# Three edits to the order of copies, sums and loads in a linear-attention plus feed-forward kernel

## The chip, the cores and the metric

The kernel runs on one core of one Trainium2 chip. The metric is the device time of one execution in microseconds (us); lower is better. Times below are from the runs of the kernel before the change and from the hardware profile of one of its executions.

## The reference

Inputs are q, k and v of shape (4, 8, 768, 64): 4 batches, 8 heads, 768 tokens, 64 channels. Two weight matrices follow, `w_in` (512 x 2048) and `w_out` (2048 x 512). All are float32. Cut to what matters:

```python
# linear attention with one decay gamma[h] per head
for t in range(768):
    state = gamma * state + k[:, :, t] outer v[:, :, t]
    y[:, :, t] = (q[:, :, t] @ state) / 8
# 4*768 = 3072 tokens, 8*64 = 512 channels
x = y.transpose(0, 2, 1, 3).reshape(3072, 512)
h = maximum(x @ w_in, 0)
out = (h * h) @ w_out            # (3072, 512)
```

## The kernel before, in words

**Chunks and blocks.** The tokens are cut into 24 chunks of 128. In the attention, a chunk's scores (its keys against its queries, masked) are multiplied with v, and the state of all earlier chunks is added. q and k are scaled by powers of gamma beforehand, so that the recurrence becomes plain products. The result of a chunk, transposed, is `xt`, the input of the feed-forward part. That part works on blocks: `BLOCKS = [4, 2, 2, ...]` gives block 0 four chunks and the ten others two each. The code calls a block `tb`.

**Products of a block.** First `psf <- xt, w_in_bf` (line 850), eight or sixteen matmuls into one PSUM tile. Then ScalarE (ACT in the profile) writes `h` with a ReLU out of PSUM (line 859), and VectorE (DVE) squares it in place (line 830, or ACT at line 828). Last come the products with `w_out`.

**Seven products instead of eight.** For blocks 1 to 10, and for the second half of block 0, the products with `w_out` are made as a 2 x 2 split with seven half-size products (Winograd's variant of Strassen's method). DVE makes sums of quarters of the squared `h`, called `s1` to `s4`; sums of quarters of `w_out` (`t1` to `t4`, the tiles `w_sum`) are made once. The products go to the accumulators `pa`, `pb`, `pd` and `pe`. `a` is a copy of `pa`'s first product. `u` is `pb + a`, `v` is the same after a further product has been added to `pb`, and the output halves are built from these by DVE adds or ACT copies into the tiles `osb` (`oa` and `ob` in the code). `seven_products` does this for blocks 1 and up; its `add` is line 883 and its matmuls are line 887. `last_of_first` does it for tokens 256 to 511 of block 0; its `add` is line 1007 and its matmuls are line 1011. There `pa` and `pe` are the two halves of one PSUM tile, `pd` and `pb` of another. Tokens 0 to 255 of block 0, chunks 0 and 1, are multiplied plainly (line 1045) into the two tiles `ops`; `store(c)` copies `ops[c]` to an `osb` tile on ACT (line 1073) and issues its output DMA on the queue of SyncE (SP, line 1074).

In `last_of_first`, the copy of `pa`'s final sum into `oa` is line 1086. In `seven_products`, `s4` lies in the space of `h` for block 1 (the tile is called `h2` and shows as `h<-h,h`) and in the tile `v_bd0` for later blocks (`v_bd<-h,k_bd`). Only `last_product` reads `s4`; it is put off into the next block (`kept`), where one step multiplies and two steps store.

**Who decides the order.** Nothing is scheduled by a planner. Each engine runs its instructions in the order of the program. The feed-forward part is a row of generators; every `yield` is a "place" with a number. At each place, `before(n)` runs the attention steps that `put(place, step, ...)` has placed there. A block of two chunks has 16 places. The waits between engines are semaphores that the framework sets from the tiles that instructions read and write.

**Attention from chunk 8 on** (`attend2`). With `d` the place of a chunk's outputs, a pair of chunks' q is loaded at `d - 29` (`load_q`, line 94), scaled at `d - 19` and `d - 18` by DVE (`scale_q`, line 390, `qs<-qn`), and transposed by DMA at `d - 16` (line 446). v is scaled at `d - 9` by DVE (`scale_v2`, line 721, shown as `v<-stage,kf`) and copied by GpSimd (POOL, line 729); k is transposed by DMA at `d - 13` (line 735). State products (`c_ps`, line 778) come at about `d - 6` and `d - 3`, scores (`st`, line 751) at `d - 5`, outputs (`y`, lines 800 and 807) at `d`. Chunks 4 to 7 take an older path: k is transposed on TensorE (line 433) and copied to `k_bd` by ACT (line 440), scores are line 459 with their mask on DVE at line 466, state copies are lines 510 (ACT) and 512 (DVE), and outputs are lines 527 and 535.

**Loads of q.** `load_q(m, heads)` issues one DMA on SP for each part of the heads that it is given. Two parts are given for chunks 6, 8 and 10, and one part, all eight heads, for chunks 12, 14, 16, 18, 20 and 22:

```python
for part in heads:
    src = q[b, part, i * C : (i + 2) * C, :].rearrange("h (s r) d -> s h r d", r=2)
    nc.sync.dma_start(t[:, part], src)
```

Of the kernel before, what the change touches and what calls it, by code (L numbers as in the profile page):

```python
# [14 lines left out]
ALU = mybir.AluOpType  # L15
# [16 lines left out]
def kernel(  # L32
# [12 lines left out]
    B, H, S, D = q.shape  # L45
# [51 lines left out]
    heads_of = [slice(0, H // 2), slice(H // 2, H)]  # L97
# [766 lines left out]
    def seven_products(tb):  # L864

        h = h2s[tb][0].rearrange("e (j k) (c t) -> e k c j t", k=2, c=2)
        a11, a12, a21, a22 = h[:, 0, 0], h[:, 1, 0], h[:, 0, 1], h[:, 1, 1]
        s1, s2, s4 = (
            t.rearrange("s p hh d -> s (p hh d)").rearrange("s (j t) -> s j t", t=C)
            for t in (k_bds[0], k_bds[1], v_bds[0])  # L870
        )
        if tb == 1:
            room = hpool.tile([P, 4096], BF16, name="h2").rearrange("e (n j t) -> e n j t", n=4, t=C)
            s1, s2, s4 = (room[:, n] for n in range(3))
        s3 = a21
        t1, t2, t3, t4 = sums
        b11, b21, b22 = (
            lambda j, k=k, n=n: w_out_bf[j // 2][:, 2 * (j % 2) + k, n * HN : (n + 1) * HN]
            for k, n in ((0, 0), (1, 0), (1, 1))
        )  # L880

        def add(out, in0, in1, op=ALU.add):
            nc.vector.tensor_tensor(out=out, in0=in0, in1=in1, op=op)  # L883

        def product(to, left, right, js, start, stop):
            for j in js:
                nc.tensor.matmul(  # L887
                    to,
                    lhsT=left[:, j],
                    rhs=right(j) if callable(right) else right[:, j],  # L890
                    start=(start and j == 0),
                    stop=(stop and j == NFB // 2 - 1),
                    skip_group_check=True,
                )

        def first_sums(js):
            add(s1[:, js], a21[:, js], a22[:, js])
            add(s2[:, js], s1[:, js], a11[:, js], ALU.subtract)

        def rest():  # L900
            first_sums(slice(4, 8))
            pa = (ps_f if tb == 1 else ps_tp).tile([P, HN], FP32, name="psf" if tb == 1 else "tp")
            pb, pe, pd = (ps_f.tile([P, HN], FP32, name="psf") for _ in range(3))
            oa, ob = (opool.tile([P, DM], FP32, name="osb") for _ in range(2))
            a, u, v = (upool.tile([P, HN], FP32, name=f"u{i}") for i in range(3))
            r0 = first[tb] * C
            for js, stop in ((range(0, 6), False), (range(6, 8), True)):
                product(pa[:], a11, b11, js, True, stop)
                product(pe[:], a22, t4, js, True, stop)
                if stop:  # L910
                    nc.scalar.activation(a[:], pa[:], AF.Copy)
                yield
            add(s3, a11, a21, ALU.subtract)
            product(pd[:], s1, t1, range(8), True, True)
            yield
            add(s4, a12, s2, ALU.subtract)
            product(pb[:], s2, t2, range(8), True, True)
            add(u[:], pb[:], a[:])
            yield
            for js in (range(0, 4), range(4, 8)):  # L920
                product(pa[:], a12, b21, js, False, js[-1] == 7)
                if js[0]:
                    nc.scalar.activation(oa[:, 0:HN], pa[:], AF.Copy)  # L923
                yield
            for js in (range(0, 4), range(4, 8)):
                product(pb[:], s3, t3, js, False, js[-1] == 7)
                if js[0]:
                    add(v[:], pb[:], a[:])
                    add(ob[:, HN:DM], pd[:], v[:])
                    add(ob[:, 0:HN], pe[:], v[:])  # L930

                    def last_product():
                        product(pd[:], s4, b22, range(8), False, True)
                        add(oa[:, HN:DM], pd[:], u[:])
                        yield
                        nc.sync.dma_start(out[r0 + C : r0 + 2 * C], ob[:])
                        yield
                        nc.sync.dma_start(out[r0 : r0 + C], oa[:])
                        yield

                    kept.append(last_product())
                yield

        def rest_at_end():
            first_sums(slice(4, 8))
            pe, pb, pd = (ps_f.tile([P, HN], FP32, name="psf") for _ in range(3))
            pa, p2 = ps_tp.tile([P, HN], FP32, name="tp"), ps_st.tile([P, HN], FP32, name="st")
            p7 = ps_y.tile([P, HN], FP32, name="y")
            oa, ob = (opool.tile([P, DM], FP32, name="osb") for _ in range(2))
            a, u, v = (upool.tile([P, HN], FP32, name=f"u{i}") for i in range(3))  # L950
            r0 = first[tb] * C
            for js, stop in ((range(0, 6), False), (range(6, 8), True)):
                product(pa[:], a11, b11, js, True, stop)
                product(pe[:], a22, t4, js, True, stop)
            nc.scalar.activation(a[:], pa[:], AF.Copy)
            yield
            add(s3, a11, a21, ALU.subtract)
            product(p2[:], a12, b21, range(0, 4), True, False)
            product(pb[:], s2, t2, range(8), True, True)
            add(u[:], pb[:], a[:])  # L960
            yield
            add(s4, a12, s2, ALU.subtract)
            product(p7[:], s3, t3, range(8), True, True)
            add(v[:], p7[:], u[:])
            add(ob[:, 0:HN], pe[:], v[:])
            yield
            product(pd[:], s1, t1, range(8), True, True)
            add(u[:], pd[:], u[:])
            add(ob[:, HN:DM], pd[:], v[:])
            nc.sync.dma_start(out[r0 + C : r0 + 2 * C], ob[:])  # L970
            yield
            product(p2[:], a12, b21, range(4, 8), True, True)
            add(oa[:, 0:HN], p2[:], a[:])
            for c in range(2):
                cols = slice(c * C, (c + 1) * C)
                p3 = (ps_tp if c else ps_c).tile([P, C], FP32, name="tp" if c else "c_ps")
                product(p3[:], s4, lambda j: b22(j)[:, cols], range(8), True, True)
                to = slice(HN + c * C, HN + (c + 1) * C)
                add(oa[:, to], p3[:], u[:, cols])
                done = slice(HN + c * C if c else 0, HN + (c + 1) * C)  # L980
                nc.sync.dma_start(out[r0 : r0 + C, done], oa[:, done])
            yield

        return first_sums, rest if tb + 1 < len(BLOCKS) else rest_at_end

    def last_of_first():

        def halves_of(k, c):
# [6 lines left out]
        s1, s2, s4 = (  # L995
            [
                t.rearrange("e (x j t) -> e x j t", x=2, t=C)[:, x]
                for x in range(2)
            ]
            for t in (spare[:, i * HN * 4 : (i + 1) * HN * 4] for i in range(3))  # L1000
        )
# [29 lines left out]
        def second_products():  # L1031
# [39 lines left out]
            def store(c):  # L1071
                osb = opool.tile([P, DM], FP32, name="osb")
                nc.scalar.activation(osb[:], ops[c][:], AF.Copy)
                nc.sync.dma_start(out[c * C : (c + 1) * C], osb[:])
# [4 lines left out]
            product(pb, s2, t2, hi)  # L1079
            add(u[:], pb, a[:])  # L1080
            yield
            store(1)
            product(pa, a12, b(1, 0), lo, False)
            yield
            product(pa, a12, b(1, 0), hi, False)
            nc.scalar.activation(oa[:, 0:HN], pa, AF.Copy)
            yield
            product(pb, s3, t3, lo, False)
            yield
# [203 lines left out]
    def put(place, what, *args):  # L1293
        parts.setdefault(place, []).append((what, args))
# [66 lines left out]
    for m, d in zip(range(PACK_FROM, NCHUNK), done):  # L1361
        attend2(m, d, done[m - PACK_FROM - 1] if m > PACK_FROM else 0,
                *ahead.get(m, (d - 19, d - 16, d - 13, d - 9)))
        if m >= 12 and m % 2 == 0:
            put(d - 29, load_q, m)
    places = {
        (8, "k"): [26 + j // 2 for j in range(8)],
        (8, "v"): [35 + j // 2 for j in range(8)],
# [52 lines left out]
```

## Time and profile before

| what | value |
| --- | --- |
| median of 3 runs | 202.81 us (202.81 to 202.84) |
| profiled execution | 202.86 us, of which 201.09 us are its span |
| TensorE busy | 194.7 us, 2361 matmuls, 2361 weight loads |
| VectorE busy | 151.0 us, 327 instructions |
| ScalarE busy | 128.0 us, 260 instructions |
| GpSimd busy | 81.9 us, 154 instructions |
| DMA | 36.03 MB in 92299 packets, 179 GB/s mean |
| granted TensorE clock | 1.00 throughout |

In the profile, PE is TensorE's matmuls and PEld its weight loads, which overlap them; DVE is VectorE, ACT ScalarE, POOL GpSimd, SP SyncE. A line of a timeline gives the start, the time from the first start to the last end, the engine, the line of the code, the operation, the tile written and the tiles read, the shape, and how many instructions are merged; brackets give the idle time of the engine before it and what ended it. A line of the DMA issues gives the tiles, the issuing queue, how often, the size of one and the median time from issue to landing. Matmuls are pipelined: one starts before the end of the one before it is recorded.

### The profile page before, as it was taken

How to read it: one execution, taken by the hardware profiler on the slowest of the kernel's cores; microseconds unless marked ns; L12 is line 12 of the kernel's file. 1: busy time of each engine (PE TensorE's matmuls, PEld its weight loads, DVE VectorE, ACT ScalarE, POOL GpSimd, SP SyncE). 2: the span in 40 equal slices, each digit the busy share in tenths (PEclk: the TensorE clock that was granted, in tenths of full speed). 3: DMA queues.
4: the chain of work that ended last, by engine and by line, in shares of the span. 5: the costliest groups of instructions: out<-in, count | busy, mean ns of one | idle time of the engine just before them, and what ended most of it. 6: DMA issues, size and time to landing. Idle time of an engine off the chain costs nothing.

```text
span 201.1 us, 5856 instructions
## 1 busy us (share of the span) xinstructions
PE 194.7 (97%) x2361; PEld 164.6 (82%) x2361; DVE 151.0 (75%) x327; ACT 128.0 (64%) x260; POOL 81.9 (41%) x154
## 2 busy tenths in 40 slices
PE   7799999999999999999999999999999999999992
PEld 2478445779988999899999999999999999999881
DVE  3987899799698896687697697697696696484472
ACT  8885875264853676774766866864865865845710
POOL 8664760899930762154522185116362202200000
PEclk9999999999999999999999999999999999999999
DMA  5999999999988999598998399989899552101102
GB/s 168 355 375 397 345 191 193 231 229 224 313 176 190 169 229 177 165 138 177 186 181 188 115 169 231 210 195 132 148 175 182 173 93 65 71 0 51 56 0 106
DMA packets 92299, 36.03 MB, mean 179 GB/s; under 512 B 68592, under 2 KB 88304, under 8 KB 92272
## 3 DMA queue, kind: packets, MB, share of 16 engines
q1 hardware_dynamic: 73136, 31.47, 65.1%
q0 software_dynamic: 19136, 4.20, 23.0%
q8 instruction: 18, 0.29, 0.6%
q14 instruction: 9, 0.07, 0.1%
HBM read 27.26 MB, written 6.29 MB: 167 GB/s over the span
## 4 chain that ended last, share of the span: by engine, by line
PE 91%; DVE 3%; DMA 2%; ACT 1%; issue 1%; DVEq 0%
PE psf L850 42%; PE psf L887 21%; PE tp L887 7%; PE psf L1045 3%; PE psf L1011 2%; DMA qn<-in_q_dram 2%; PE st L751 2%; PE y L807 2%; PE y L800 2%; PE c_ps L778 2%; PE c_ps L656 1%; PE y L535 1%; PE st L459 1%; DVE qs L562 1%; PE y L371 1%
## 5 line engine op out<-in xcount | busy, mean ns | idle before, releaser
L850 PE MATMUL psf<-xt,w_in_bf 128*128 128x256 bf16 (+2 forms) x864 | 92.3, 261 | 0.0
L850 PEld LDWEIGHTS <-w_in_bf 128*128 128x128 bf16 x864 | 70.7, 98 | 11.2
L859 ACT ACTIVATE h<-psf 128x512 bf16<-128x512 f32 x96 | 56.3, 595 | 23.5 <-PE psf L850 21.2
L729 POOL COPY v_bd<-v 64x512 bf16<-64x512 bf16 x32 | 21.7, 677 | 76.2 <-DVE v L721 75.3
L830 DVE TENSOR_TENSOR h<-h 128x512 bf16<-128x512 bf16 x80 | 33.0, 428 | 18.5 <-ACT h L859 18.1
L887 PEld LDWEIGHTS <-h 128*128 128x128 bf16 x344 | 31.7, 98 | 3.7 <-issue 0.2
L157 POOL DMA_DIRECT2D k_big<-in_k_dram x40 | 26.6, 686 | 0.0
L887 PE MATMUL psf<-w_sum,h 128*128 128x256 bf16 x168 | 23.5, 273 | 0.0
L887 PE MATMUL tp<-w_out_bf,h 128*128 128x256 bf16 x136 | 19.1, 273 | 0.0
L887 PE MATMUL psf<-w_sum,k_bd 128*128 128x256 bf16 x144 | 17.9, 273 | 0.0
L883 DVE TENSOR_TENSOR u<-psf,u 128x256 f32<-128x256 f32 x20 | 8.5, 424 | 12.3 <-PE psf L887 11.4
L883 DVE TENSOR_TENSOR osb<-psf,u 128x256 f32<-128x256 f32 x29 | 11.5, 421 | 6.6 <-PE psf L887 6.3
L887 PEld LDWEIGHTS <-k_bd 128*128 128x128 bf16 x144 | 13.8, 98 | 1.5
L787 ACT ACTIVATE s_bd<-c_ps 64x256 bf16<-64x256 f32 x29 | 10.7, 369 | 6.3 <-PE c_ps L778 6.3
L390 DVE TENSOR_TENSOR qs<-qn,qf 128x512 bf16<-128x512 f32 x20 | 13.7, 690 | 0.0
L788 ACT ACTIVATE s_bd<-c_ps 64x256 bf16<-64x256 f32 x29 | 11.0, 379 | 0.4
L721 DVE TENSOR_TENSOR v<-stage,kf 128x512 bf16<-128x512 f32 x16 | 10.9, 684 | 0.3 <-issue 0.3
L758 DVE TENSOR_TENSOR pt<-st,cmask 128x512 bf16<-128x512 f32 x16 | 11.0, 688 | 0.2
L923 ACT ACTIVATE osb<-tp 128x256 f32<-128x256 f32 x8 | 3.1, 384 | 12.2 <-PE tp L887 12.2
L814 ACT ACTIVATE xt<-y 128x512 bf16<-128x512 f32 x16 | 9.6, 598 | 1.8 <-PE y L807 1.2
L828 ACT ACTIVATE h<-h 128x512 bf16<-128x512 bf16 x16 | 10.1, 629 | 0.5
L883 DVE TENSOR_TENSOR k_bd<-h 128x512 bf16<-128x512 bf16 x18 | 9.9, 552 | 0.3
(148 smaller groups left out, 290.0 us busy)
## 6 DMA issues: line engine op xcount, KB each, us to landing
out_dram<-osb SPq DMA_DIRECT2D x23, 256.0 KB, 2.5
qn<-in_q_dram SPq DMA_DIRECT2D x9, 512.0 KB, 5.4
stage<-in_v_dram SPq DMA_DIRECT2D x32, 96.0 KB, 4.0
stage<-in_moe_w_in_dram SPq DMA_DIRECT2D x4, 512.0 KB, 6.8
stage<-in_moe_w_in_dram SPq DMA_DIRECT2D x2, 1024.0 KB, 10.7
w_out_bf<-in_moe_w_out_dram POOLq DMA_DIRECT2D x4, 512.0 KB, 10.2
kn<-in_k_dram SPq DMA_DIRECT2D x6, 256.0 KB, 5.7
qn<-in_q_dram SPq DMA_DIRECT2D x6, 256.0 KB, 5.8
```

Of the source, the lines that this page charges most:

```text
L157: nc.gpsimd.dma_start(t[rows, 2 * at_w : 2 * (at_w + size), p, hh, :], half_rows(k, b, 2 * p + hh, i + w, size),)
L390: engine.tensor_tensor(out=out, in0=by, in1=table[:, :, None].to_broadcast([P, H, D]), op=ALU.mult)
L721: nc.vector.tensor_tensor(out=v2.rearrange("s (u p) d -> s u p d", u=2), in0=vn, in1=kf2[:, i, :, :, None].to_broadcast([P, 2, NPAIR, D]), ...
L729: nc.gpsimd.tensor_copy(v_bd[rows, :, hh, :], v2[rows])
L758: nc.vector.tensor_tensor(out=pt[:], in0=st[:], in1=cmask2.rearrange("s r t -> s (r t)")[:, None, :].to_broadcast([P, 2 * NPAIR, C // 2]), ...
L787: nc.scalar.activation(s_bd[halves[0], :, 0, :], c[halves[0]], AF.Copy)
L788: nc.scalar.activation(s_bd[halves[1], :, 1, :], c[halves[1]], AF.Copy)
L830: nc.vector.tensor_mul(hv, hv, hv)
L850: nc.tensor.matmul(hp, lhsT=w_in_bf[g][:, cb, fq * 128 : (fq + 1) * 128], rhs=xts[tb][:, cb, cols], start=(cb == 0), stop=(cb == NCB - 1),)
L859: nc.scalar.activation(hv, hp[:], AF.Relu)
L883: nc.vector.tensor_tensor(out=out, in0=in0, in1=in1, op=op)
L887: nc.tensor.matmul(to, lhsT=left[:, j], rhs=right(j) if callable(right) else right[:, j], start=(start and j == 0), stop=(stop and j == NF ...
```

## The change

There are three edits. In `seven_products`, the sum `s4` is made one step later, behind `pb`'s product, the add of `u` and a `yield`. In `last_of_first`, `store(1)` moves one step later, behind the two parts of `pa`'s last product and the copy of `pa`. q of chunks 12 to 20 is loaded with two DMAs of four heads each; that of chunk 22 still with one.

```diff
@@ seven_products, rest() @@
             add(s3, a11, a21, ALU.subtract)
             product(pd[:], s1, t1, range(8), True, True)
             yield
-            add(s4, a12, s2, ALU.subtract)
             product(pb[:], s2, t2, range(8), True, True)
             add(u[:], pb[:], a[:])
             yield
+            add(s4, a12, s2, ALU.subtract)
             for js in (range(0, 4), range(4, 8)):
                 product(pa[:], a12, b21, js, False, js[-1] == 7)
@@ last_of_first, second_products() @@
             product(pb, s2, t2, hi)
             add(u[:], pb, a[:])
             yield
-            store(1)
             product(pa, a12, b(1, 0), lo, False)
             yield
             product(pa, a12, b(1, 0), hi, False)
             nc.scalar.activation(oa[:, 0:HN], pa, AF.Copy)
+            store(1)
             yield
             product(pb, s3, t3, lo, False)
@@ placing of the attention steps @@
         if m >= 12 and m % 2 == 0:
-            put(d - 29, load_q, m)
+            put(d - 29, load_q, m, heads_of if m < 22 else (slice(0, H),))
```

On the engines' queues this does the following. ACT has `pa`'s copy ahead of chunk 1's copy. DVE has `s4` behind `u` in blocks 1 to 9: in block 1 also behind the mask of a chunk's scores and a copy of the state, in block 2 also behind a scaling of v, in blocks 3 to 8 ahead of that scaling. SP issues five DMAs more; the stores keep their places among its other instructions. The matmuls keep their order.

## The prediction

> **What bounds the kernel now.** I read the page's busy times first, then the chain that ended last, then the timeline of single engines wherever TensorE (PE) did not start matmuls back to back.
>
> ```profile
> span 201.1 us, 5856 instructions
> PE 194.7 (97%) x2361; PEld 164.6 (82%) x2361; DVE 151.0 (75%) x327; ACT 128.0 (64%) x260; POOL 81.9 (41%) x154
> PE 91%; DVE 3%; DMA 2%; ACT 1%; issue 1%; DVEq 0%
> ```
>
> PE is the bound: 97% busy and 91% of the chain, at a granted clock of 1.00. The view by windows gives PE 15.00 of every 15.00 us from 75 to 195 us and 14.98 from 60 to 75. But "busy" hides short stops. A 256-column matmul is recorded with 273 ns, while the chain gives 0.87 us to eight of them, so one can start every 0.109 us; PE may pause some 0.16 us and still look busy. The pauses must be read from starts. After the first 21 us there are only two that the edits can reach; each is followed by the engine that ended it.
>
> First, the timeline around 44 us, in the last part of the first block:
>
> ```profile
> 44.20 0.49 PE L459 MATMUL st<-qT,k_bd 128*128 128x128 bf16 x4
> 44.32 0.60 ACT L1073 ACTIVATE osb<-psf 128x512 f32<-128x512 f32 x1
> 44.53 1.31 PE L1011 MATMUL psf<-w_sum,h 128*128 128x256 bf16 x8
> 44.73 0.69 DVE L466 TENSOR_TENSOR pt<-st,cmask 128x512 bf16<-128x512 f32 x1 [0.27 <-PE st L459]
> 44.82 0.38 ACT L1086 ACTIVATE osb<-psf 128x256 f32<-128x256 f32 x1
> 45.25 0.31 PEld L1011 LDWEIGHTS <-h 128*128 128x128 bf16 x3 [0.29 <-issue]
> 45.68 0.39 PE L459 MATMUL st<-qT,k_bd 128*128 128x128 bf16 x4
> ```
>
> Eight L1011 matmuls take 1.31 us here and 1.04 at 41.79. Four (pb) start at 44.53 and every 0.109 after; the next four (pe) are due at 44.97 and start at 45.25. They share a PSUM tile with pa, whose copy is L1086, and that copy stands on ScalarE (ACT) behind the 0.60 us of chunk 1's copy, L1073. It ends at 45.20, and PE goes on at 45.25.
>
> Second, 61 us, the seven products of block 1:
>
> ```profile
> 61.09 0.69 DVE L883 TENSOR_TENSOR h<-h,h 128x1024 bf16<-128x1024 bf16 x1
> 61.09 1.05 PE L887 MATMUL psf<-w_out_bf,h 128*128 128x256 bf16 x8
> 61.69 0.42 DVE L883 TENSOR_TENSOR u<-psf,u 128x256 f32<-128x256 f32 x1
> 62.02 0.68 DVE L466 TENSOR_TENSOR pt<-st,cmask 128x512 bf16<-128x512 f32 x1
> 62.16 0.60 PE L887 MATMUL psf<-w_sum,h 128*128 128x256 bf16 x4
> ```
>
> The eight on pa start at 61.09 and the last at 61.87 (61.09 + 1.05 - 0.27). The next group writes pb again, is due at 61.98 and starts at 62.16: it must wait until u has been read out of pb (62.11). That u stands on VectorE (DVE) right behind the 0.69 us of s4, the first row.
>
> **The change, part by part.** *Chunk 1's copy behind pa's.* Each is one ACT instruction; none is added. pa's copy now follows k_bd (which ends at 44.30), so it runs 44.32 to 44.70, before PE is due at 44.97. Gain: 45.25 - 44.97 = 0.28. What is late next is DVE: the second scores (45.68 before) would come at 44.97 + 4 x 0.109 = 45.40, but they overwrite st, which the mask add reads until 44.73 + 0.69 = 45.42. From DVE's end to PE's start the trace shows 0.05 (u 62.11 to 62.16), so they start at 45.48: 0.08 given back, net 0.20. Further on, PE arrives 0.20 earlier than before: its transposes of the second half of qs are due at 46.82 against qs ready at 46.62, the last product at 47.94 against pd's reader ending at 47.76. Both hold. Chunk 1's copy now ends near 45.24; its PSUM buffer is wanted by the second group of block 1's first products at 47.04, its store on the SP queue is not reached before 45.78, and its place there is unchanged. The next work on ACT starts at 47.00. So nothing waits for it.
>
> *s4 one step later, block 1.* u starts where s4 did, at 61.09 (its product ends before 60.7), and ends at 61.51, well ahead of PE. Gain 0.18. The mask add and the copy behind it come earlier too; s4 runs near 62.5 and is first read at 65.48.
>
> *s4, blocks 2 to 9.* No PE pause is there to win, so the cover is what counts. In block 2, and in block 9 which loads no v, nothing urgent stands behind s4. In blocks 3 to 8 the v of a later chunk does (rows of block 4):
>
> ```profile
> 105.64 0.69 DVE L883 TENSOR_TENSOR v_bd<-h,k_bd 128x1024 bf16<-128x1024 bf16 x1
> 106.58 0.42 DVE L883 TENSOR_TENSOR u<-psf,u 128x256 f32<-128x256 f32 x1 [0.26 <-PE psf L887]
> 106.92 0.68 DVE L721 TENSOR_TENSOR v<-stage,kf 128x512 bf16<-128x512 f32 x1
> 108.53 0.28 PE L778 MATMUL c_ps<-v,k_big 128*128 128x64 bf16 x4
> 108.73 0.43 DVE L883 TENSOR_TENSOR u<-psf,u 128x256 f32<-128x256 f32 x1 [1.12 <-PE psf L887]
> ```
>
> s4 (first row) moves to 106.92, so v starts 0.60 later, at 107.52, and ends at 108.20. L778 multiplies that v at 108.53. With 0.05 to get there 0.28 is left: no cost, but a thin cover. The v sum at 108.73 waits for PE in any case, and POOL's copies of v, 0.60 later, are read at 115.1. The last product reads s4 at 110.6.
>
> *q by halves, five times.* Bytes and 512-byte pieces stay; SP issues five DMAs more. An issue of half a q takes 0.58 (two in 1.17 at 57.83), of a whole one 0.57 to 0.64, so what stands behind on SP (v loads, transposes of k) comes up to 0.6 later:
>
> ```profile
> qn<-in_q_dram SPq DMA_DIRECT2D x9, 512.0 KB, 5.4
> stage<-in_v_dram SPq DMA_DIRECT2D x32, 96.0 KB, 4.0
> qn<-in_q_dram SPq DMA_DIRECT2D x6, 256.0 KB, 5.8
> kT<-k_big SPq DMA_TRANSPOSE x16, 4.3
> ```
>
> The tightest q is the one issued at 104.68: whole, it lands 4.9 later, at 109.6, and is scaled at 112.04. Scaling needs both halves, so nothing is won either. From below the second half costs nothing (the pairs at 57.83 landed after 3.8 each); from above it takes 7.3, as the pair at 42.85 did: 105.3 + 7.3 = 112.6, against 112.04 less 0.385. DVE idles 0.48 before 113.20 and 0.79 before 115.62, which takes up that lateness. I take zero. The k transpose behind it (106.33) is wanted only at 118.6.
>
> Sum: 0.20 + 0.18, with unrounded rows 0.385 us. The profiled execution took 202.86, of which 201.09 span and 1.77 around it; it would become 202.48. The median of the runs is 202.81, 0.05 below, which gives **202.42**. From 62.2 us on PE has no pause that could take the gain back, and the last block's tail hangs on PE's end.
>
> **The rivals.** *More is won.* Two short waits stand beside the two: k_bd's second half holds PE 0.10 at 44.35, and a square of h about 0.07 at 57.45. If the wait at 45.48 does not arise (0.08), or one of these shrinks as the engines realign, the time is 202.25 to 202.35. For: DVE and ACT there follow PE. Against: k_bd itself is not moved.
>
> *Only one gain stays.* If u is held by something that the rows do not name, or DVE, almost without idle time from 53 to 62 us, does not follow the 0.20, one term drops out: 202.61 or 202.63; both gone, 202.81. This is also the case in which an edit doesn't do what it says.
>
> *v too late (slower).* Place: L778 in blocks 3 to 8. It decides once DVE loses over 0.28 between u and the end of v. For: at 92.49, where v waits for seven DMAs, the trace has 0.33 idle ahead of it. Against: it is there once only, and runs beside u. Were it behind s4 in all six blocks, v would start 0.33 after s4's end instead of 0.09 before, and reach PE at 108.67: 0.14 each, 0.84 in all, 202.42 + 0.84 = 203.27.
>
> *q too late (slower).* Were the second half to take 11.5, the longest of the L94 loads, it would land at 116.8, 5.1 late, and 1.27 idle would leave 3.9 on the path: 206.3. Against: from 71 us on these loads take 4.9 to 6.0. The Trainium skill speaks for it: "DMA: Bandwidth & Descriptors", section "Anatomy of one DMA", gives every transfer a fixed 2.0 us or so besides its bytes. Counted whole, that is an estimate of 109.6 + 0.6 + 2.0 = 112.2 for the second half, which would still leave the sum as it is. The pairs at 57.83 show no such doubling.
>
> **How the numbers follow.** Both stops gone, 202.42 to within 0.05: 0.62. More won: 0.20. One or both terms lost: 0.10. v late 0.05, q late 0.03. A change of 0.2%, about what a measurement of this kernel can tell from none, is 0.41 us, the time 202.40: the main case lies on that edge, and I split it 0.30 below and 0.32 above. Faster: 0.30 + 0.20 = 0.50; same: 0.32 + 0.10 = 0.42; slower: 0.08. The range leaves out the slow cases and the outermost of the others: 202.22 to 202.75.
>
> **What would show it.** Right: ACT has pa's copy before the second L1073, the eight L1011 matmuls at 44.53 take 1.04, the second scores start near 45.48, pb's matmuls follow those on pa without a pause near 61.8, every later stage lies 0.385 earlier, span 200.70; in blocks 3 to 8 v starts 1.0 after u and L778 has no wait; 16 q loads of 256 KB and four of 512. Wrong: a pause ahead of L778, an idle DVE ahead of qs, a new wait between 46 and 57 us, or a tail that doesn't move.

## The result and the profile after

| | before | after |
| --- | --- | --- |
| median of 5 runs each | 202.82 us | 202.01 us (201.93 to 202.05) |
| ratio | | 0.9957 (95%: 0.9946 to 0.9968) |
| profiled execution | 202.86 us | 201.93 us |
| its span | 201.09 us | 200.14 us |
| start of the last matmul | 196.95 us | 196.76 us |

The change saves 0.81 us where 0.39 was forecast, and the time lies below the range. The last two rows say that most of it is not where the forecast looked for it: the last matmul comes only 0.19 earlier, the end of the span 0.95. All ratios here are those on record, worked out from the runs and not from the medians; some kernels have a few runs 0.3 to 1.6 us longer than their others, so a ratio need not be the quotient of the medians.

The page after, span and chain, and then the page's rows of the loads:

```profile
span 200.1 us, 5858 instructions
PE 194.7 (97%) x2358; PEld 164.8 (82%) x2361; DVE 150.4 (75%) x327; ACT 128.0 (64%) x260; POOL 82.5 (41%) x154
PE 93%; DVE 3%; DMA 2%; issue 1%; ACT 0%; DVEq 0%
...
qn<-in_q_dram SPq DMA_DIRECT2D x16, 256.0 KB, 4.6
...
qn<-in_q_dram SPq DMA_DIRECT2D x4, 512.0 KB, 5.8
```

PE still carries the chain. (Three matmul records are missing, x2358 against x2361. Each leaves what looks like a pause of 0.216 us, one 512-column matmul, at 20.3, 31.1 and 39.8; the matmuls after them are not late.) The same two places as in the forecast, from the timeline:

```profile
44.17 0.49 PE L459 MATMUL st<-qT,k_bd 128*128 128x128 bf16 x4
44.29 0.38 ACT L1085 ACTIVATE osb<-psf 128x256 f32<-128x256 f32 x1
44.50 1.04 PE L1011 MATMUL psf<-w_sum,h 128*128 128x256 bf16 x8
44.57 0.59 ACT L1073 ACTIVATE osb<-psf 128x512 f32<-128x512 f32 x1
44.70 0.69 DVE L466 TENSOR_TENSOR pt<-st,cmask 128x512 bf16<-128x512 f32 x1 [0.27 <-PE st L459]
45.45 0.38 PE L459 MATMUL st<-qT,k_bd 128*128 128x128 bf16 x4
...
60.86 1.05 PE L887 MATMUL psf<-w_out_bf,h 128*128 128x256 bf16 x8
61.19 0.68 DVE L466 TENSOR_TENSOR pt<-st,cmask 128x512 bf16<-128x512 f32 x1
61.74 0.60 PE L887 MATMUL psf<-w_sum,h 128*128 128x256 bf16 x4
```

pa's copy (L1085 now) runs first, the eight L1011 take 1.04, and the second scores start at 45.45 behind the mask add. At 61.74 pb's matmuls follow those on pa at once (60.86 + 8 x 0.109). Up to here the forecast holds to the hundredth: a matmul at 67 us lies 0.414 earlier, 0.03 of it from the first microseconds of this one execution.

Then two losses. Chunks 12 and 18, timelines of before, and of after (`v_bd<-h,k_bd` is s4, L721 makes v, L778 multiplies it):

```profile
92.49 0.69 DVE L721 TENSOR_TENSOR v<-stage,kf 128x512 bf16<-128x512 f32 x1 [0.33 <-issue]
93.67 0.28 PE L778 MATMUL c_ps<-v,k_big 128*128 128x64 bf16 x4
...
136.74 0.68 DVE L721 TENSOR_TENSOR v<-stage,kf 128x512 bf16<-128x512 f32 x1
138.34 0.28 PE L778 MATMUL c_ps<-v,k_big 128*128 128x64 bf16 x4
```

```profile
92.26 0.68 DVE L721 TENSOR_TENSOR v<-stage,kf 128x512 bf16<-128x512 f32 x1
93.26 0.39 PE L778 MATMUL c_ps<-v,k_big 128*128 128x64 bf16 x4
...
136.44 0.68 DVE L883 TENSOR_TENSOR v_bd<-h,k_bd 128x1024 bf16<-128x1024 bf16 x1
137.04 0.69 DVE L721 TENSOR_TENSOR v<-stage,kf 128x512 bf16<-128x512 f32 x1
138.04 0.39 PE L778 MATMUL c_ps<-v,k_big 128*128 128x64 bf16 x4
```

Four L778 matmuls take 0.39 instead of 0.28 in these two chunks, and 0.28 as before in the others. From the end of v to the first of them it was 0.49 and 0.92 before; it is 0.32 in both after. Asked for line 778 between 92 and 95 us, the trace after says why (PEldq is the queue of PE's weight loads):

```profile
L778 PEldq EVENT_SEMAPHORE  x4: 51/51/51, 93.0 to 93.4; - x4
L778 PEld LDWEIGHTS <-k_big x4: 95/97/98, 93.2 to 93.4; 128*128 128x128 bf16 x4
```

PE's queue has four instructions here that only wait, one ahead of each weight load. k_big is freshly loaded for these two chunks, by eight DMAs with a semaphore each, and the first product of such a load waits for all of them. PE's queue runs ahead of the matmuls, but its first wait is also for v: v is done 0.32 ahead of the first L778, the wait is passed 0.04 later, and by the records the next ones follow 0.125 apart, where matmuls of this size without them follow 0.029 apart. The fourth comes 0.10 after the first L778 has started: 0.11 lost, twice. (Chunks 8, 15 and 21 have such waits too, but their v ends 1.5 us ahead or more.) So the last matmul is 0.414 - 0.112 - 0.112 = 0.19 earlier.

The other 0.76 is behind the last matmul. Line 1416 is the end of the kernel, where SP waits for all DMAs. SP's instructions of that line (durations in ns as least, median, most; first and last start), before:

```profile
L1416 SPq EVENT_SEMAPHORE  x11: 17/28/28, 198.1 to 201.0; - x11
L1416 SPq DRAIN  x3: 7/7/13, 200.2 to 200.6; - x3
```

and after:

```profile
L1416 SPq EVENT_SEMAPHORE  x11: 17/28/28, 197.9 to 200.1; - x11
L1416 SPq DRAIN  x3: 7/7/13, 199.3 to 199.6; - x3
```

From the view of SP's own waits, what it waited for the stores there (us in total, times, longest), before and after:

```profile
SPq L1416 <- DMA out_dram<-osb: 1.2, 3, 0.6
```

```profile
SPq L1416 <- DMA out_dram<-osb: 0.5, 2, 0.3
```

The last store lands at 199.44 and 199.22, 0.22 apart. SP's first drain, from which the rest of the end follows in 0.84 in both, comes at 200.25 and 199.30. From the landing to the drain it is 0.81 before and 0.08 after. What lies between is in the records of SP's waits. There are nine in a fixed order, each for two semaphores; their starts are

```
before 198.11 198.71 199.20 199.46 199.55 199.62 200.04 200.12 200.18, drain 200.25
after  197.91 198.32 198.40 198.46 198.53 198.59 198.65 198.99 199.24, drain 199.30
```

SP's DMAs signal on eight semaphores in turn, which are waited for second to ninth. Before, the last three stores have the second, third and fourth: behind the landing SP still passes five waits that have long been fulfilled, 0.06 to 0.09 apart, and among them is a pause: the seventh starts 0.42 behind the sixth. With five DMAs more, the last three stores have the seventh, eighth and ninth, and the pause stands ahead of the second: all of it passes while the stores are under way.

### The profile page after: what moved, and what is told of

It reads as the page before. It is cut to its first block, busy times and chain, and to the rows that moved or that the text cites. A ratio compares the mean times of both kernels' runs of the same rounds, so it can differ in the third digit from the quotient of the medians.

```text
span 200.1 us, 5858 instructions
## 1 busy us (share of the span) xinstructions
PE 194.7 (97%) x2358; PEld 164.8 (82%) x2361; DVE 150.4 (75%) x327; ACT 128.0 (64%) x260; POOL 82.5 (41%) x154
## 4 chain that ended last, share of the span: by engine, by line
PE 93%; DVE 3%; DMA 2%; issue 1%; ACT 0%; DVEq 0%
PE psf L850 42%; PE psf L887 21%; PE tp L887 7%; PE psf L1045 3%; PE psf L1011 3%; DMA qn<-in_q_dram 2%; PE y L807 2%; PE st L751 2%; PE c_ps L778 2%; PE y L800 2%; PE c_ps L656 1%; PE st L459 1%; PE y L535 1%; DVE qs L562 1%; PE y L371 1%
## 5 line engine op out<-in xcount | busy, mean ns | idle before, releaser
L721 DVE TENSOR_TENSOR v<-stage,kf 128x512 bf16<-128x512 f32 x16 | 10.9, 684 | 0.0
```

The lines of the kernel that those rows point to most:

```text
L721: nc.vector.tensor_tensor(out=v2.rearrange("s (u p) d -> s u p d", u=2), in0=vn, in1=kf2[:, i, :, :, None].to_broadcast([P, 2, NPAIR, D]), ...
```

## The experiments

Each is the kernel before with one edit, unless it says otherwise; medians are compared with those of the kernel before, timed with them on the same chip: 202.87 for the first four, 202.83 for the others.

**Only chunk 1's copy moved** (the second hunk of the change alone).

> Only chunk 1's copy is moved behind pa's copy. Theory A (each edit has its own place, the end of the kernel hangs on the number of SP's DMAs): TensorE's pause of 0.28 at 44.97 is gone and 0.08 comes back ahead of the second scores; every later matmul lies 0.20 earlier, no pause in L778 of chunks 12 and 18, and from the last store's landing to SP's first drain it stays about 0.8 as before: 202.82 - 0.20 = 202.62. Rival B (the end is shorter because TensorE ends earlier, whatever the DMAs): the 0.72 at the end comes too, 201.9.

Measured: 202.68, 0.19 less (ratio 0.9994, 0.9982 to 1.0007, which alone would not tell it from nothing). The trace does: from 45.48 us on every matmul is 0.203 earlier, L778 is as before, landing to drain takes 0.80. Theory A; the end does not follow from an earlier TensorE.

**Only s4 moved** (the first hunk alone).

> Only s4 is made one step later, in blocks 1 to 9. Theory A: the 0.18 at 61.98 is won, and 0.11 is lost in L778 of chunk 12 (93.7) and again of chunk 18 (138.3), where four waits of 0.125 each stand between v and TensorE's weights: the last matmul comes 0.04 later than before, 202.86; the end as before. Rival C (the 0.11s come from the loads by halves or from the 0.20 of the copy, not from s4): 202.82 - 0.18 = 202.64, no pause in L778.

Measured: 202.92, 0.05 more (1.0003, 0.9991 to 1.0015). The profiled execution took 203.94; 0.93 of its excess lies ahead of 21 us and 0.08 at 47 us, so only distances are read from it: no pause at pb's matmuls in block 1, and 0.39 for the four L778 of chunks 12 and 18. What s4 wins in block 1 it loses there. Rival C falls.

**Only the loads by halves** (the third hunk alone).

> Only q of chunks 12 to 20 by halves. Theory A: no matmul moves; the last three stores signal on the three semaphores that SP waits for last, and a pause of 0.36 among these waits lies ahead of the landing and not behind it; from the last landing to SP's first drain 0.08 instead of 0.81: 202.82 - 0.72 = 202.10. Rival B: the end as before, 202.82. Rival D (the prediction's slower case, q too late): above 203.

Measured: 202.13, 0.74 less (0.9959, 0.9945 to 0.9974). The last matmul starts at 196.96, as before (196.95). SP's instructions at the end:

```profile
L1416 SPq EVENT_SEMAPHORE  x11: 17/28/28, 198.1 to 200.3; - x11
L1416 SPq DRAIN  x3: 7/7/13, 199.5 to 199.8; - x3
```

Landing to drain is 0.08 with the stores no earlier. So the loads by halves bring nine tenths of what the change brings, and they do it as five more DMAs.

**s4 moved in blocks 3 and 6 alone.**

```diff
-            add(s4, a12, s2, ALU.subtract)
+            if not (tb in (3, 6)):
+                add(s4, a12, s2, ALU.subtract)
             product(pb[:], s2, t2, range(8), True, True)
             add(u[:], pb[:], a[:])
             yield
+            if tb in (3, 6):
+                add(s4, a12, s2, ALU.subtract)
```

> s4 is made one step later in blocks 3 and 6 alone, those whose v belongs to chunks 12 and 18; everything else as before. Theory A: nothing is won and 0.11 is lost twice, in L778 at 93.7 and 138.5: 203.04. Rival C: no pause in L778, 202.82.

Measured: 203.10, 0.23 more (1.0013, 1.0001 to 1.0026). The timeline around the two products:

```profile
93.68 0.39 PE L778 MATMUL c_ps<-v,k_big 128*128 128x64 bf16 x4
...
138.46 0.39 PE L778 MATMUL c_ps<-v,k_big 128*128 128x64 bf16 x4
```

0.11 is lost at each, and the last matmul is 0.22 later, as much as s4's move costs behind block 1 in the kernel with s4 moved everywhere (0.23): these two places are the whole price of s4's move in blocks 2 to 9.

**s4 moved in block 1 alone, beside the other two edits.** The changed kernel with the condition `tb == 1` in place of `tb in (3, 6)` above.

> The changed kernel, but with s4 one step later in block 1 alone, where a pause is won, and where it was in blocks 2 to 9. Theory A: both pauses ahead of 62 us are gone, no pause in L778 of chunks 12 and 18, the end as in the changed kernel: its 202.01 less 2 x 0.11 = 201.79. Rival: s4 costs something in other blocks too, below 201.7, or the 0.22 comes back elsewhere, 202.0.

Measured: median 201.73 of 7, 1.10 less than the kernel before (ratio 0.9956, 0.9940 to 0.9971). The median is 0.28 below the changed kernel's, which was timed on another occasion; between the two traces the last matmul comes 0.21 earlier (196.55 against 196.76). The trace has neither the two pauses ahead of 62 us nor those in L778 (0.28 in both chunks), and the end is short (SP's drains; three lines more move line 1416 to 1419):

```profile
L1419 SPq DRAIN  x3: 7/7/13, 199.1 to 199.4; - x3
```

This version is faster than the kernel before and has the lowest median of all; that it beats the changed kernel rests on the two traces and on medians of different occasions.

The last three separate what is at work at the end.

**Three DMAs fewer**, `put(15, load_q, 6)` and so on, without `heads_of`, for chunks 6, 8 and 10.

> The kernel before, with q of chunks 6, 8 and 10 loaded whole: three DMAs fewer on SP instead of five more. Eight semaphores are used in turn, so the last three stores signal on the same three as in the changed kernel. Theory A (two parts: the turn of the semaphores, and a pause of 0.35 that stands at a fixed count of SP's instructions): nothing waits behind the landing except the pause, which now comes three instructions later, ahead of the first drain: landing to first drain 0.08 + 0.35 = 0.43, time 202.82 - 0.38 = 202.44. The turn alone (no fixed count): 0.08, 202.10. The count alone: 0.81 or more, 202.8.

**Six by halves**, `put(d - 29, load_q, m, heads_of)` for all of chunks 12 to 22.

> The kernel before, with q of chunks 12 to 22 by halves: six DMAs more on SP. The very last store now signals on the semaphore that is waited for second of nine. Theory A: the pause of 0.35 comes ahead of the first wait, hidden beside the transfer; behind the landing stand seven waits of some 0.065 each: landing to first drain 0.45 + 0.08 = 0.53, time 202.82 - 0.28 = 202.54. The turn alone: some 0.9, 202.9. More DMAs as such are good: 202.1 or less.

**Eight pieces more.**

```diff
-            put(d - 29, load_q, m)
+            put(d - 29, load_q, m, heads_of if m > 14 else (slice(0, 4), slice(4, 6), slice(6, 8)))
```

> The kernel before, with q of chunks 12 and 14 in three pieces and of 16 to 22 in two: eight DMAs more, so the last stores signal on the same semaphores as before. Theory A: five waits behind the landing as before, but without the pause: landing to first drain 0.45 instead of 0.81. The pause stands eight instructions earlier, ahead of the wait of the very last store, whose issue it puts off by up to 0.36: time between 202.46 and 202.82, likelier the upper end. The turn alone: 0.81 and 202.82, with no later store.

Measured, with the semaphores of the last three stores by their places in SP's nine waits, and the pause, read from the records:

| kernel | SP's DMAs | last stores wait at | pause ahead of | landing to drain, expected | measured | median against before |
| --- | --- | --- | --- | --- | --- | --- |
| before | 0 | 2, 3, 4 | 7th wait | | 0.81 | |
| three fewer | -3 | 7, 8, 9 | first drain | 0.43 | 0.42 | -0.26 |
| five halves | +5 | 7, 8, 9 | 2nd wait | 0.08 | 0.08 | -0.74 |
| six halves | +6 | 8, 9, 2 | 1st wait | 0.53 | 0.52 | -0.28 |
| eight pieces | +8 | 2, 3, 4 | the last store's wait | 0.45 | 0.39 | +0.36 |

(Ratios of the three: 0.9999, 0.9989 to 1.0010; 0.9988, 0.9973 to 1.0003; 1.0014, 1.0006 to 1.0023. The first was expected at 202.44 and came at 202.57; the drain into which the pause falls takes 0.14 instead of 0.01 there. The profiled execution of the second took 202.88, with a pause at 48 us that no other trace has; only its end is read.) SP's drains with three fewer, and SP's waits for the stores with six halves:

```profile
L1416 SPq DRAIN  x3: 7/7/136, 199.8 to 200.3; - x3
```

```profile
SPq L1416 <- DMA out_dram<-osb: 0.9, 1, 0.9
```

With six halves there is one wait of 0.9 for the very last store, at the second place, and seven fulfilled ones behind it. The kernel with three fewer has the stores on the same semaphores as the changed one and lacks only the shift of the pause: 0.39 of the 0.73 is the turn of the semaphores (0.81 to 0.42), 0.34 is the pause (0.42 to 0.08). That more DMAs as such help is refuted by six and eight. In all five kernels the pause stands at the same count of SP's instructions, ahead of the 208th in its records: it moved by exactly the DMAs added or taken away.

The kernel with eight pieces went wrong for one reason that was expected and one that was not. The pause put off the last store's issue from 197.66 to 198.00. But that store also took longer (DMA view of the end: size, us from issue to landing):

```profile
out_dram<-osb SPq DMA_DIRECT2D x1, 64.0 KB, 2.2
```

2.2 from issue to landing against 1.8 before, which gives the 0.4 that the expectation lacks. The records of its packets say where: of the store's 16 landings 15 come by 199.68, the last at 200.20. Of its 128 packets 120 start by 199.14. The last eight start one behind another from 199.37 on, when a packet of 8192 bytes on the queue that the profile calls "instruction", running from 199.04, has just ended; in the other four kernels of the table that packet starts only when the store's packets are through. So the likely cause is that this packet held up the store's share on one DMA engine. It is not shown: the records don't name the engine, and no run was made for it.

What the pause is, no run shows. The Trainium skill ("Runtime: NRT & Kernel Launch", section "Instruction fetch mechanics") says that each engine's sequencer loads its instructions in blocks of a fixed size by a DMA queue of its own, and that crossing into the next block is mostly hidden. A fixed count of instructions fits that, and the packet of 8192 bytes on the profile's queue "instruction" starts 0.6 to 1.1 after the pause in each of these traces. If the pause is such a crossing, "mostly hidden" does not hold for SP here: the step from wait to wait is 0.06, and 0.42 at that place.

## Why the prediction was wrong

**Chunk 1's copy: right.** Forecast 0.20 with the new wait at 45.48; alone it moved every later matmul by 0.203, and the second scores started at 45.48.

**s4 in block 1: right.** The pause of 0.18 is gone in every kernel that has this edit, and nothing came in its place.

**s4 in blocks 2 to 9: wrong in two of eight blocks.** The step that failed is "With 0.05 to get there 0.28 is left: no cost, but a thin cover". v's end was placed well (0.33 ahead of L778 forecast, 0.32 measured). What was wrong is the 0.05 from v to PE: it came from a place with one wait. In chunks 12 and 18 four waits 0.125 apart stand there, and from v's end to the last of them it is 0.42. The cost was 2 x 0.11 instead of nothing. The rival "v too late" named the right line, but by another mechanism (v behind s4) and in all six blocks. (Its 202.42 + 0.84 is 203.26, not 203.27; nothing hangs on that.) The waits could have been seen before: asked for line 778, the trace of before has

```profile
L778 PEldq EVENT_SEMAPHORE  x4: 51/51/51, 93.2 to 93.6; - x4
```

between 92 and 95 us. The Trainium skill has the rule ("Perfetto Trace Analysis", section "Identifying Dependency Chains"): an instruction that waits for several engines may have extra semaphore instructions put ahead of it. The trace agrees, with the semaphores of several loads in the place of engines, and adds the price, a step of 0.125 on PE's queue for each.

**q by halves: right about q, wrong about the edit.** This is the term of the sum that was wrong: taken at zero, it measured -0.74 alone. "Scaling needs both halves, so nothing is won" held: no matmul moved. (The section of the Trainium skill that the rival "q too late" names gives its fixed 2.0 us for DMAs that GpSimd issues, while q is loaded by SP; the estimate of 112.2 did not enter the sum.) "I take zero" counted the five issues against what stands behind them on SP's queue, and stopped at the last store. The step that failed is "the last block's tail hangs on PE's end". It does so only as far as the last store's landing (with chunk 1's copy alone both came 0.20 earlier). Behind that it hangs on SP: on which semaphores the last stores have, and on how many instructions SP has run. The forecast took in neither, though SP's waits before showed 1.2 us in three waits at line 1416, and the drain 0.81 behind the last landing.

**The sum.** Forecast: -0.385. Between the two profiled executions: -0.385 in the two pauses, -0.03 in the first microseconds, +0.22 in L778, -0.73 from landing to drain, -0.03 in the stores' issue and landing, and +0.02 outside the span: -0.93. The medians differ by 0.81, and the three edits alone add up to -0.19 + 0.05 - 0.74 = -0.88. The 0.07 between them is less than the 0.12 by which the changed kernel's five runs differ.

The chance of 0.50 for faster was borne out, but by a term that no case held. "More is won" pointed to 44 to 57 us, where the waits of 0.07 and 0.10 stayed as they were.

## What to carry to other kernels

An edit that adds or drops a DMA can change the end of a kernel, however early it is made: look at which semaphores the last stores get and at the order in which they are waited for, and make the last store the last in it. A cover of 0.3 us is to be compared with all the waits ahead of the instruction, one by one, above all for the first reader of freshly loaded data. And of an edit that is good in one block and bad in others, only the good part need be kept: this gave the lowest median here.

## What the runs showed of the hardware

A wait that is already fulfilled costs its queue time: a step of some 0.062 us on SP's queue, and on PE's one of 0.125, with a weight load and a matmul in it that alone take 0.029. Behind the last landing, five such waits and one pause were worth 0.73 us, 0.36% of this kernel, more than both pauses of the bounding engine together.
